# Second products of the last block with w2 as the stationary operand and 512 tokens streamed

## The chip, the cores and the metric

One Trainium2 chip, one of its cores. The metric is the device time of one execution in microseconds, the median of several runs.

## The reference, cut to what matters

Linear attention (its output is `x`, 2304 tokens by 512) and then a dense mixture of four experts:

```python
p = domain_probs / (domain_probs.sum(-1, keepdims=True) + 1e-09)
out = np.zeros((N, D), dtype=np.float32)          # 2304 x 512
for e in range(E):                                 # 4 experts
    h = np.maximum(x @ w1[e], 0.0)                 # 512 -> 1024
    out += p[:, e:e + 1] * (h @ w2[e])             # 1024 -> 512
```

All of it is float32. Each factor of a product is kept as a high and a low part of a narrower type (`hh`, `hl`), and a product is the sum of three: high by high, and the two mixed ones.

## The kernel before

The tokens go in blocks through the experts. The last block has 1024 tokens (`BIG[2]`, tokens 1280 to 2303); it makes eight visits (`DEEP`), each to one half (512 hidden features) of one expert. Attention is over by then. In this block both matrix products of a visit are cut into two by two parts, and seven products of parts stand for eight (Strassen's scheme in Winograd's form); the sums of parts that it needs are made by the other engines.

A visit, in the function `fast` with `deep` true:

- First products (`product`, L991, matmul at L999). The hidden features of the visit come in two halves `g` of 256, and for each there are seven products `p` of w1's parts with the token halves: six matmuls each (two slices of the sum, three pairs of high and low), w1 stationary in the array, 512 tokens streamed. The result is 128 features by 512 tokens in one PSUM bank. There are 84 matmuls a visit.
- Sums and relu. Some products are copied to SBUF by ScalarE (`keep`, L1005) and added by VectorE to later ones (`both`, L1013). The result goes through relu into the high part `hh` (ScalarE, L1023, L1057) and the low part `hl` (VectorE, L1029, L1060: relu and difference in one instruction). For the second seven products, differences of relu outputs are needed (`less`, L989, tiles `t1`, `t2` and `r11`), which are split into high and low by ScalarE and GpSimd (`split`, L630, L633).
- Second products (`sevens` at L1079, `seventh` at L1072, matmul at L1077). Here the hidden values are stationary, 128 tokens at a time, and 256 columns of w2 (or of sums of its parts, `w2s`) are streamed: each of the seven products has four token quarters `q`, two features slices `f` and three pairs, 24 matmuls of 256 columns, 168 a visit. Four banks `X` hold the left and right half of an output, two banks `Z` the third product. A result is 128 tokens by 256 output columns.
- `gather` (L830) adds a result to the output kept in SBUF (`acc`): VectorE multiplies by the share `pr` of the expert, which is one number for each partition (a token), and adds (L847; at first L843). In the last visit `finished` (L852) stores each piece of 128 by 256 at once.

Around this run, in the order in which they are written: the splits of w2's parts and of their sums for this and the next visit (`prepare`, `on_sides2`, on ScalarE and GpSimd), the loads of w2 (`load_deep`, L624, on SP's queue) and the loads of the next w1 parts from a kept copy (on GpSimd's queue). PSUM has eight banks, given out by `bank`. All engines work through their instructions in the order in which the function writes them; semaphores are put in for every dependence, and where two engines touch one PSUM bank, also between two readers.

Of the kernel before, what the change touches and what calls it, by code (L numbers as in the profile page):

```python
# [6 lines left out]
F32 = mybir.dt.float32  # L7
# [7 lines left out]
def attention_moe(ctx, tc, kT, qT, kd, qd, kn, qn, vn, omT, probs, w1, w2, out):  # L15
# [31 lines left out]

    raw_x = xs.tile([P, NP, RING], F32, tag="raw_x", name="raw_x")
# [60 lines left out]
    wide = {}  # L109
    cut = slice(D - 1, D - 1 + VW)  # L110
# [202 lines left out]
    class Halves(Pair):  # L313
# [87 lines left out]
        def turn(self, part):  # L401
# [7 lines left out]
            if part:  # L409
                pt = bank("qt_ps")[:, :P]  # L410
                nc.tensor.transpose(pt, self.qx[2][:, 0], ident)
                pieces.append((pt.rearrange("p (j t) -> p j t", j=2), slice(2 * P, 2 * P + D)))
# [409 lines left out]
    begun_at = set()  # L822

    def part(i, cs):
        if not isinstance(acc[i], list):
            return acc[i][:, cs]
        h = cs.start // H
        return acc[i][h][:, cs.start - h * H:cs.stop - h * H]

    def gather(v, ps, t, cs=slice(0, DM)):  # L830
        _, e, _, c0, n = visits[v]
        i = c0 // P + t
        sc = pr[:, i, e:e + 1]
        if i not in acc:
            if v in DEEP and t == 3:
                acc[i] = [att.tile([P, H], F32, tag=x, name="acc", bufs=1) for x in ("kvh", "kvl")]
            else:
                acc[i] = held([P, DM], "acc", F32)
        to = part(i, cs)
        fresh = [h for h in (0, H) if cs.start <= h < cs.stop and (i, h) not in begun_at]  # L840
        begun_at.update((i, h) for h in fresh)
        if fresh and v in DEEP:
            nc.vector.tensor_scalar(to, ps, sc, None, ALU.mult)  # L843
        elif fresh:
            nc.scalar.activation(to, ps, AF.Copy, scale=sc)
        else:
            nc.vector.scalar_tensor_tensor(to, ps, sc, to, ALU.mult, ALU.add)  # L847

    def finished(v, t, cs):
        if v + 1 == len(visits):  # L850
            i = visits[v][3] // P + t
            nc.sync.dma_start(out[i * P:(i + 1) * P, cs], part(i, cs))  # L852
# [104 lines left out]
    def fast(v):  # L957
# [3 lines left out]
        deep = v in DEEP  # L961
        hs = [tuple(held([P, n if deep else 2 * n], x) for x in ("hh", "hl")) for _ in range(FH)]
# [3 lines left out]
        ready2 = iter(())  # L966
# [3 lines left out]
        if deep:  # L970
            if v == DEEP[0]:
                sevens_t.append(xs.tile([P, 5, 2, n], F32R, tag="raw_x", name="t_hl"))
                for _ in range(2):
                    on_sides2(v)
            B, ready2 = sides2.pop(v)
            steps2 = [1, 0, 1, 0, 1, 1, 1, 0] if v == DEEP[0] else [1, 1, 1, 0, 0, 1, 1, 0]
            T1, A22 = ((sevens_t[0][:, i], sevens_t[0][:, i + 1]) for i in (0, 2))
            t1, t2 = (x.rearrange("p t c -> p (t c)")[:, :2 * n].rearrange("p (k x) -> p k x", k=2) for x in (va, vb))
            r11 = att.tile([P, 2, n], F32, tag="q", name="r11", bufs=1)

        def prepare():
            if deep:
                for _ in range(steps2.pop(0)):
                    next(ready2, None)
            else:
                split_w2()

        def less(to, t, x, op=ALU.subtract):
            nc.vector.scalar_tensor_tensor(to, t, 0.0, x, ALU.max, op)  # L989
# [19 lines left out]
        def both(g, f, j, where, name, hold=False):  # L1009
            t, kept = P_[g][where], P_[g][name]  # L1010
            if not deep or where == "u":
                t = kept
            nc.vector.tensor_tensor(t, P_[g][where], kept, ALU.add)  # L1013
            P_[g][name] = t
            if deep and j == 1:
                if g == 0:
                    if f == 0:
                        less(t1[:, 0], t, r11[:, 0])
                    return
                ha, hc = (x[:, f] for x in A22)  # L1020
            else:
                ha, hc = (x[:, j * n:(j + 1) * n] for x in hs[2 * g + f])
            nc.scalar.activation(ha, t, AF.Relu)  # L1023
            if deep and g == f == j == 0:
                nc.scalar.activation(r11[:, 0], t, AF.Relu)
            lows.append((hc, t, ha))
            if not (hold and not deep):
# [26 lines left out]
        def p4(g):  # L1054
# [3 lines left out]
            if deep and g == 0:  # L1058
                nc.scalar.activation(r11[:, 1], P_[0]["u"], AF.Relu)
# [12 lines left out]
        def seventh(q, to, a, b, start=True, fs=(0, 1)):  # L1072
            for f in fs:
                (xa, xc), (wa, wc) = a[f], b[f]
                xa, xc = (x[:, q * P:(q + 1) * P] for x in (xa, xc))
                for k, (x, w) in enumerate(((xa, wa), (xa, wc), (xc, wa))):
                    nc.tensor.matmul(to, x, w, start=(start and f + k == 0), stop=(f + k == 3), skip_group_check=not start)  # L1077

        def sevens():  # L1079

            L, R, Q = slice(0, H), slice(H, DM), range(4)

            def split_of(t):
                return [tuple(x[:, f] for x in t) for f in range(2)]

            def weights(g, cs):
                return [tuple(x[:, cs] for x in W[v, "w2", 2 * g + f]) for f in range(2)]

            def mixed(i, cs):
                return [tuple(x[:, cs] for x in B[f, i]) for f in range(2)]  # L1090

            X, Z = [], []
            for f in range(2):
                for q in Q[:2]:
                    if f == 0:
                        X.append(bank("g2"))
                    seventh(q, X[q][:, L], hs[:2], weights(0, L), fs=(f,))
            p7(1)
            less(t2[:, 1], P_[1]["p5"], t1[:, 1])
            for q in Q[2:]:  # L1100
                X.append(bank("g2"))
                seventh(q, X[q][:, L], hs[:2], weights(0, L))
            split(t2[:, 1], *hs[1], nc.scalar, nc.gpsimd)
            p3(1)
            p4(1)
            less(t2[:, 0], P_[1]["u2"], t1[:, 0])
            split(t2[:, 0], *hs[0], nc.scalar, nc.gpsimd)
            nc.gpsimd.tensor_tensor(r11, t2, r11, ALU.subtract)
            for q in Q:
                seventh(q, X[q][:, R], split_of(T1), mixed(1, R), start=False)  # L1110
            for q in Q:
                gather(v, X[q][:, L], q, L)
                gather(v, X[q][:, R], 4 + q, R)
            yield 2
            zs = []
            for q in Q:
                if q % 2 == 0:
                    Z.append(bank("g2"))
                zs.append(Z[q // 2][:, q % 2 * H:(q % 2 + 1) * H])
                seventh(q, zs[q], hs[2:], weights(1, L))  # L1120
            for f in range(2):
                split(r11[:, f], *hs[2 + f], nc.scalar, nc.gpsimd)
            yield 2
            for q in Q:
                seventh(q, X[q][:, R], split_of(A22), mixed(1, L), start=False)

            def second(q):
                gather(v, zs[q], q, L)
                finished(v, q, L)

            def third(q):
                gather(v, X[q][:, R], 4 + q, L)

            less(t1[:, 1], P_[1]["u"], t2[:, 1])
            less(t1[:, 0], P_[1]["p1"], t2[:, 0])
            for q in Q:
                third(q)
            for q in Q[:2]:
                second(q)
            split(t1, *T1, nc.scalar, nc.gpsimd)  # L1140
            next(ready, None)
            next(ready, None)
            on_sides2(v + 1)
            yield 1
            for q in Q:
                seventh(q, X[q][:, L], hs[:2], mixed(0, L), start=False)
                gather(v, X[q][:, L], 4 + q, L)
                finished(v, 4 + q, L)
                if q < 2:
                    second(2 + q)  # L1150
            next(ready, None)
            on_sides2(v + 1)
            on_sides2(v + 1)
            yield 1
            for q in Q:
                seventh(q, X[q][:, L], hs[2:], mixed(0, R), start=False)
                gather(v, X[q][:, L], 4 + q, R)
                finished(v, 4 + q, R)
# [6 lines left out]
            for t in range(tiles):  # L1165
                gathered(v, t)
# [386 lines left out]
```

## Time and profile before

| | us |
|---|---|
| median of 3 runs (lowest, highest) | 879.42 (878.98, 879.53) |
| the profiled execution | 879.01 |
| its span, first to last instruction | 877.2 |
| TensorE busy | 871.1 (99%), granted clock 1.00 |
| weight loads busy | 785.1 (90%) |
| VectorE, ScalarE, GpSimd busy | 568.1, 477.9, 563.9 |
| the last block, eight visits and the end | 560.4 to 877.2 |

The profile is of one execution. A busy time is a sum over an engine's instructions; matmuls overlap, so TensorE's says only that something was in flight. A wait is the idle time of an engine ahead of an instruction, put down to the one that released it last.

### The profile page before, as it was taken

The numbers are of one execution on the slowest core, as the hardware profiler recorded it, in microseconds if no ns is written. First come the engines' busy times: TensorE is split into PE (matmuls) and PEld (weight loads), VectorE is DVE, ScalarE is ACT, GpSimd is POOL, SyncE is SP. The second block draws the span as 40 slices with busy tenths as digits, with TensorE's granted clock in tenths as the row PEclk, the third lists the DMA queues.
The fourth block names the chain that finished last, engine by engine and source line by source line (L and its number), as shares of the span: only waits on it lengthen the run. The fifth ranks groups of instructions, "written<-read, shape, count | busy, mean of one in ns | idle before, by whom it ended". The sixth has DMA issues, their size and how long they took to land.

```text
span 877.2 us, 14757 instructions
## 1 busy us (share of the span) xinstructions
PE 871.1 (99%) x5456; PEld 785.1 (90%) x5456; DVE 568.1 (65%) x1001; ACT 477.9 (54%) x1075; POOL 563.9 (64%) x518
## 2 busy tenths in 40 slices
PE   9999999999999999999999999999999999999997
PEld 9988888989888898988989989898989899998987
DVE  5666566666678547566675666975847567574846
ACT  6696677776774555555555554544443434444341
POOL 6859474655644454444453436879888897889864
PEclk9999999999999999999999999999999999999999
DMA  7664534624421955645466255635144442515222
GB/s 183 194 211 159 204 111 155 187 77 144 159 73 49 314 182 202 232 139 192 142 214 226 82 197 227 214 112 180 44 174 121 131 136 81 171 47 180 80 89 97
DMA packets 64296, 134.01 MB, mean 153 GB/s; under 512 B 10368, under 2 KB 20800, under 8 KB 64224
## 3 DMA queue, kind: packets, MB, share of 16 engines
q1 hardware_dynamic: 54256, 102.95, 35.3%
q0 software_dynamic: 9360, 29.82, 10.4%
q8 instruction: 43, 0.70, 0.4%
q10 hardware_dynamic: 608, 0.30, 0.1%
q14 instruction: 29, 0.24, 0.1%
HBM read 98.96 MB, written 34.08 MB: 152 GB/s over the span
## 4 chain that ended last, share of the span: by engine, by line
PE 98%; DVE 1%; DMA 0%; issue 0%; ACT 0%; SPq 0%
PE g L999 31%; PE g L1077 18%; PE g L818 9%; PE g L819 8%; PE g L820 8%; PE g L803 3%; PE g L804 3%; PE g L805 3%; PE kv L396 2%; PE k_ps L341 2%; PE q_ps L341 1%; PE qt_ps L407 1%; PE k_ps L148 1%; PE q_ps L148 1%; PE nd L280 1%; PE kv L183 1%
## 5 line engine op out<-in xcount | busy, mean ns | idle before, releaser
L847 DVE SCALAR_TENSOR_TENSOR acc<-g,pr,acc 128x256 f32<-128x256 f32 (+1 forms) x278 | 140.2, 542 | 42.8 <-PE g L820 27.6
L633 POOL TENSOR_TENSOR w2l<-w2r,w2h 128x512 fp32r<-128x512 f32 x61 | 79.3, 1309 | 76.7 <-ACT w2h L630 66.4
L633 POOL TENSOR_TENSOR w1sl<-w1r,w1sh 128x512 fp32r<-128x512 f32 (+1 forms) x43 | 75.2, 1749 | 59.5 <-ACT w1sh L630 53.2
L818 PE MATMUL g<-w2h,hh 128*128 128x512 f32 x280 | 111.6, 399 | 0.0
L820 PE MATMUL g<-w2h,hl 128*128 128x512 f32 x280 | 109.6, 391 | 0.0
L819 PE MATMUL g<-w2l,hh 128*128 128x512 f32 x280 | 109.5, 391 | 0.0
L999 PE MATMUL g<-xbh,w1sh 128*128 128x384 f32 (+1 forms) x256 | 93.0, 363 | 0.0
L999 PE MATMUL g<-xbl,w1sh 128*128 128x384 f32 (+1 forms) x256 | 92.9, 363 | 0.0
L999 PE MATMUL g<-xbh,w1sl 128*128 128x384 f32 (+1 forms) x256 | 92.6, 362 | 0.0
L1005 ACT ACTIVATE sum<-g 128x384 f32<-128x384 f32 (+1 forms) x96 | 52.1, 543 | 69.5 <-PE g L999 68.6
L633 POOL TENSOR_TENSOR w1al<-w1r,w1ah 128x512 fp32r<-128x512 f32 (+1 forms) x45 | 49.5, 1116 | 59.6 <-ACT w1ah L630 56.2
L999 PE MATMUL g<-xbh,w1ah 128*128 128x384 f32 (+1 forms) x192 | 69.9, 364 | 0.0
L999 PE MATMUL g<-xbl,w1ah 128*128 128x384 f32 (+1 forms) x192 | 69.6, 362 | 0.0
L999 PE MATMUL g<-xbh,w1al 128*128 128x384 f32 (+1 forms) x192 | 69.5, 362 | 0.0
L1013 DVE TENSOR_TENSOR sum<-g,sum 128x384 f32<-128x384 f32 (+1 forms) x64 | 37.4, 587 | 44.1 <-PE g L999 38.8
L820 PEld LDWEIGHTS g<-w2h,hl 128*128 128x128 f32 x280 | 52.5, 188 | 11.5 <-DVE hl L810 0.2
L818 PEld LDWEIGHTS g<-w2h,hh 128*128 128x128 f32 x280 | 52.6, 188 | 10.2
L819 PEld LDWEIGHTS g<-w2l,hh 128*128 128x128 f32 x280 | 52.6, 188 | 8.9
L999 PEld LDWEIGHTS g<-xbh,w1sh 128*128 128x128 f32 x256 | 48.1, 188 | 5.7 <-DVE sum L1013 0.6
L999 PEld LDWEIGHTS g<-xbl,w1sh 128*128 128x128 f32 x256 | 48.1, 188 | 5.2
L1023 ACT ACTIVATE hh<-sum 128x384 fp32r<-128x384 f32 x48 | 25.0, 524 | 50.7 <-DVE sum L1013 50.3
L999 PEld LDWEIGHTS g<-xbh,w1sl 128*128 128x128 f32 x256 | 48.1, 188 | 5.1
(234 smaller groups left out, 2485.6 us busy)
## 6 DMA issues: line engine op xcount, KB each, us to landing
w1r<-in_w SPq DMA_DIRECT2D x54, 512.0 KB, 3.7
w2r<-in_w SPq DMA_DIRECT2D x76, 256.0 KB, 3.1
kept<-w1sh SPq DMA_DIRECT2D x16, 512.0 KB, 4.8
kept<-w1sl SPq DMA_DIRECT2D x16, 512.0 KB, 5.3
w1sh<-kept POOLq DMA_DIRECT2D x16, 512.0 KB, 4.8
w1sl<-kept POOLq DMA_DIRECT2D x16, 512.0 KB, 5.7
kept<-w1ah SPq DMA_DIRECT2D x16, 384.0 KB, 4.7
kept<-w1al SPq DMA_DIRECT2D x16, 384.0 KB, 4.8
```

Source lines behind the costliest of these rows:

```text
L341: nc.tensor.matmul(ps[j][:, i * P:(i + 1) * P], t[rows, c:c + P], om_r[rows], start=True, stop=True)
L633: lo.tensor_tensor(c, t, f32(a), ALU.subtract)
L803: nc.tensor.matmul(ps[:, :n], a[:, w], hi, start=(hp == 0), stop=False)
L804: nc.tensor.matmul(ps[:, :n], a[:, w], lo, start=False, stop=False)
L818: nc.tensor.matmul(ps, ha[:, ts_], wa, start=(c == 0), stop=False)
L819: nc.tensor.matmul(ps, ha[:, ts_], wc, start=False, stop=False)
L820: nc.tensor.matmul(ps, hc[:, ts_], wa, start=False, stop=(c == FH - 1))
L847: nc.vector.scalar_tensor_tensor(to, ps, sc, to, ALU.mult, ALU.add)
L999: nc.tensor.matmul(ps, a[:, w], x[:, k], start=(start and k + at == 0), stop=(k == 1 and at == 2), skip_group_check=not start)
L1005: nc.scalar.activation(t, P_[g][where], AF.Copy)
L1013: nc.vector.tensor_tensor(t, P_[g][where], kept, ALU.add)
L1077: nc.tensor.matmul(to, x, w, start=(start and f + k == 0), stop=(f + k == 3), skip_group_check=not start)
```

## The change

In the last block the second products change sides: w2's parts (128 of their columns at a time) stand in the array and the hidden values of 512 tokens are streamed. Each of the seven products has two output slices `i`, two feature slices `f` and three pairs, 12 matmuls of 512 columns, 84 a visit. A result is 128 output columns by 512 tokens; products that are added stay in two banks (`xl` or `xr`), the third has two banks `z`.

As tokens now lie along the free axis, a share can't be one number for each partition. A visit multiplies the hidden values instead: after the sums, which now stay in PSUM (two in new banks), VectorE does relu and the multiplication by a tile of shares in one instruction (`scaled`), and the high part, the low part and the differences are made from that. The share tiles (512 tokens the same in all partitions) are loaded from a small table in DRAM on SP's queue, once for each expert (`share_rows`); the table is written during attention (`turn_shares`: a transposition, a copy, a store). `into` then only adds a result to the output in SBUF. The output of this block is stored turned, in pieces of 128 by 512, and the host puts it in order.

The visit has its own function, `deep`; the other visits keep `fast` without the branches for it. The order of products, sums and preparations is that of before but for what follows: b11 is multiplied before product (1,6), the two slices of the first second product stand before and after product (1,7), `r11` is taken in two halves, and b12 and b22 are split later.

```diff
+    def share_rows(e):
+        if not shares:
+            shares.extend(held([P, 512], "w2r", F32, "share") for _ in range(2))
+        for j, t in enumerate(shares):
+            rows = pr_rows.rearrange("(j i e) p -> j e i p", j=2, e=E)[j, e]
+            nc.sync.dma_start(t.rearrange("p (i c) -> p i c", c=P), rows.partition_broadcast(P))
...
+        def added(g, where, name, to=None):
+            t = P_[g][where] if to is None else to
+            nc.vector.tensor_tensor(t, P_[g][where], P_[g][name], ALU.add)
+            return t
+        def scaled(t, j):
+            nc.vector.scalar_tensor_tensor(t, t, 0.0, shares[j], ALU.max, ALU.mult)
...
+        def high(t, to):
+            nc.scalar.activation(to, t, AF.Copy)
+        def low(t, hi, to):
+            nc.vector.tensor_tensor(to, t, f32(hi), ALU.subtract)
+        def times(to, a, b, fs=(0, 1), start=True, at=(0, 1)):
+            for f in fs:
+                (xa, xc), (wa, wc) = a[f], b[f]
+                for i in at:
+                    ps, w = to[i], slice(i * P, (i + 1) * P)
+                    for k, (y, x) in enumerate(((wa, xa), (wa, xc), (wc, xa))):
+                        nc.tensor.matmul(
+                            ps, y[:, w], x, start=(start and f + k == 0), stop=(f + k == 3), skip_group_check=not start
+                        )
+        def into(ps, j, c, at=(0, 1)):
...
+                if fresh:
+                    nc.vector.tensor_copy(t, ps[i])
+                else:
+                    nc.vector.tensor_tensor(t, ps[i], t, ALU.add)
...
+        product(1, 1, "u")
+        keep(1, "u", "p1")
+        a11 = added(0, "b2", "p1")
+        scaled(a11, 0)
+        high(a11, hs[0][0])
+        high(a11, r11[:, 0])
+        low(a11, *hs[0])
+        prepare()
+        product(1, 2, "b2")
+        a12 = added(1, "b2", "p1")
+        scaled(a12, 0)
+        high(a12, hs[2][0])
+        low(a12, *hs[2])
+        prepare()
+        product(0, 7, "u", start=False)
+        a21 = added(0, "u", "p5", bank("t"))
+        scaled(a21, 1)
...
+        product(0, 3, "b5", start=False)
+        b21 = added(0, "b5", "u2")
+        scaled(b21, 1)
+        product(0, 4, "u", start=False)
+        b11 = P_[0]["u"]
+        scaled(b11, 0)
+        high(b11, hs[1][0])
+        product(1, 6, "u", start=False)
+        keep(1, "u", "u2")
+        high(b11, r11[:, 1])
+        less(t1[:, 0], b21, r11[:, 0])
+        low(b11, *hs[1])
+        less(t1[:, 1], a21, r11[:, 1])
...
+        xl = [bank("g2") for _ in range(2)]
+        times(xl, hs[:2], weights(0, L), fs=(0,))
+        product(1, 7, "u", start=False)
+        a22 = added(1, "u", "p5", bank("t"))
+        scaled(a22, 1)
+        less(t2[:, 1], a22, t1[:, 1])
+        times(xl, hs[:2], weights(0, L), fs=(1,))
+        high(a22, A22[0][:, 1])
...
+        low(a22, A22[0][:, 1], A22[1][:, 1])
+        product(1, 3, "b5", start=False)
+        b22 = added(1, "b5", "u2")
+        scaled(b22, 1)
+        high(b22, A22[0][:, 0])
+        product(1, 4, "u", start=False)
+        b12 = P_[1]["u"]
+        scaled(b12, 0)
+        high(b12, hs[3][0])
+        less(t2[:, 0], b22, t1[:, 0])
...
+        low(b12, *hs[3])
+        low(b22, A22[0][:, 0], A22[1][:, 0])
+        xr = [bank("g2") for _ in range(2)]
+        times(xr, split_of(T1), mixed(1, R))
+        into(xr, 1, 1)
+        into(xl, 0, 0)
+        z = [bank("g2") for _ in range(2)]
+        times(z, hs[2:], weights(1, L))
...
+        times(xr, split_of(A22), mixed(1, L), start=False)
+        into(z, 0, 0)
+        done(0, 0)
+        into(xr, 1, 0)
...
+        times(xl, hs[:2], mixed(0, L), start=False)
+        into(xl, 1, 0)
+        done(1, 0)
...
+        times(xl, hs[2:], mixed(0, R), start=False)
+        into(xl, 1, 1)
+        done(1, 1)
...
+        for i in range(2):
+            times(xl, split_of(T1), weights(1, R), start=False, at=(i,))
+            into(xl, 0, 1, at=(i,))
+            done(0, 1, at=(i,))
```

## Rows read from the trace of the kernel before

**Rows 1.** Busy time by stretch, one visit: span; PE, PEld, DVE, ACT, POOL; PEclk; DMA.

```profile
599.40:638.40 39.00, 39.00 (x254) 35.66 (x253) 24.80 (x46) 16.46 (x28) 33.48 (x33) 1.00 0.39 130
```

**Rows 2.** Chain that ended last, one visit: start, length, engine, group, count.

```profile
599.56 14.99 PE g L999 x66
614.55 1.43 PE g L1077 x12
...
621.55 17.03 PE g L1077 x144
638.58 14.99 PE g L999 x66
```

**Rows 3.** VectorE in order, same visit: start, us, line, operation, [idle before <-releaser].

```profile
608.03 0.69 DVE L1029 SCALAR_TENSOR_TENSOR hl<-g,hh 128x512 fp32r<-128x512 f32 x1 [4.92 <-ACT r L1025]
608.64 0.69 DVE L1013 TENSOR_TENSOR g<-g,sum 128x512 f32<-128x512 f32 x1
609.99 0.69 DVE L1029 SCALAR_TENSOR_TENSOR hl<-g,hh 128x512 fp32r<-128x512 f32 x1 [0.66 <-ACT hh L1023]
610.60 0.68 DVE L1013 TENSOR_TENSOR sum<-g,sum 128x512 f32<-128x512 f32 x1
611.86 0.70 DVE L1013 TENSOR_TENSOR g<-g,sum 128x512 f32<-128x512 f32 x1 [0.58 <-PE g L999]
612.67 0.69 DVE L989 SCALAR_TENSOR_TENSOR va<-g,r 128x512 f32<-128x512 f32 x1
```

**Rows 4.** ScalarE in order, same visit.

```profile
606.42 0.60 ACT L1005 ACTIVATE sum<-g 128x512 f32<-128x512 f32 x1 [0.76 <-PE g L999]
...
607.39 0.60 ACT L1025 ACTIVATE r<-g 128x512 f32<-128x512 f32 x1
609.36 0.60 ACT L1023 ACTIVATE hh<-g 128x512 fp32r<-128x512 f32 x1 [1.36 <-DVE g L1013]
```

**Rows 5.** TensorE in order, same visit: the end of (0,3), the start of (0,4).

```profile
611.44 0.39 PE L999 MATMUL g<-xbh,w1sl 128*128 128x512 f32 x1
611.66 0.39 PE L999 MATMUL g<-xbh,w1ah 128*128 128x512 f32 x1
```

**Rows 6.** Groups by line and shape, last block: busy us, mean ns | idle before.

```profile
L847 DVE SCALAR_TENSOR_TENSOR acc<-g,pr,acc 128x256 f32<-128x256 f32 x208 | 89.2, 478 | 15.1 <-PE g L1077 15.1
...
L1013 DVE TENSOR_TENSOR sum<-g,sum 128x512 f32<-128x512 f32 x15 | 10.3, 686 | 11.1 <-PE g L999 11.1
...
L989 DVE SCALAR_TENSOR_TENSOR vb<-sum,va 128x512 f32<-128x512 f32 x8 | 6.0, 746 | 0.0
```

**Rows 7.** All engines in order, an earlier block: TensorE held by VectorE.

```profile
429.79 1.23 DVE L1013 TENSOR_TENSOR sum<-g,sum 128x384 f32<-128x384 f32 x2
429.91 0.33 PE L999 MATMUL g<-xbl,w1sh 128*128 128x384 f32 x1
...
430.08 0.34 PE L999 MATMUL g<-xbh,w1sl 128*128 128x384 f32 x1
...
430.39 0.19 PEld L999 LDWEIGHTS g<-xbh,w1sh 128*128 128x128 f32 x1 [0.29 <-DVE sum L1013]
...
430.68 0.34 PE L999 MATMUL g<-xbl,w1sh 128*128 128x384 f32 x1
```

**Rows 8.** VectorE in order, first visit of the last block: its first sum.

```profile
567.16 0.68 DVE L1013 TENSOR_TENSOR g<-g,sum 128x512 f32<-128x512 f32 x1
```

**Rows 9.** Waits of SP's queue, last block: total us, times, longest.

```profile
SPq L624 <- POOL w2l L633: 226.6, 7, 34.3
```

**Rows 10.** The end in order, then output stores: KB each, us to landing.

```profile
872.42 0.28 PE L1077 MATMUL g<-w2h,t_hl 128*128 128x256 f32 x1
872.74 0.48 DVE L847 SCALAR_TENSOR_TENSOR acc<-g,pr,acc 128x256 f32<-128x256 f32 x1 [0.23 <-PE g L1077]
...
out<-acc SPq DMA_DIRECT2D x10, 256.0 KB, 4.4
out<-acc SPq DMA_DIRECT2D x16, 128.0 KB, 1.9
```

More of the change, by code (lines that the diff above doesn't have):

```diff
@@ L820, in outputs, with gather @@
             nc.tensor.matmul(ps, hc[:, ts_], wa, start=False, stop=(c == FH - 1))
[L822 to L830, printed above, removed]
+    def gather(v, ps, t):
         _, e, _, c0, n = visits[v]
@@ L834, in gather @@
         if i not in acc:
[L835 to L845, printed above, removed]
-        else:
[L847 to L852, printed above, removed]
+            acc[i] = held([P, DM], "acc", F32)
+            nc.scalar.activation(acc[i], ps, AF.Copy, scale=sc)
+        else:
+            nc.vector.scalar_tensor_tensor(acc[i], ps, sc, acc[i], ALU.mult, ALU.add)
     def gathered(v, t):
@@ L960, in fast @@
         tiles, n = n // P, n // 2
-        deep = v in DEEP
-        hs = [tuple(held([P, n if deep else 2 * n], x) for x in ("hh", "hl")) for _ in range(FH)]
+        hs = [tuple(held([P, 2 * n], x) for x in ("hh", "hl")) for _ in range(FH)]
         P_ = [{}, {}]
@@ L1009, in both @@
         def both(g, f, j, where, name, hold=False):
[L1010 to L1022, printed above, removed]
+            t = P_[g][name]
+            nc.vector.tensor_tensor(t, P_[g][where], t, ALU.add)
+            ha, hc = (x[:, j * n:(j + 1) * n] for x in hs[2 * g + f])
             nc.scalar.activation(ha, t, AF.Relu)
-            if deep and g == f == j == 0:
-                nc.scalar.activation(r11[:, 0], t, AF.Relu)
             lows.append((hc, t, ha))
-            if not (hold and not deep):
+            if not hold:
                 for x, y, z in lows:
@@ L1070, in begun @@
             outputs(v, hs, g2[t], t, range(2))
[L1072 to L1158, printed above, removed]
-            on_sides2(v + 1)
-            yield 1
-            for q in Q:
-                seventh(q, X[q][:, L], split_of(T1), weights(1, R), start=False)
-                gather(v, X[q][:, L], q, R)
-                finished(v, q, R)
-            for t in range(tiles):
-                gathered(v, t)
-            yield 1
@@ L1192, in fast @@
         p5(1)
-        if deep:
-            prepare()
-            if v > DEEP[0] and v + 1 in DEEP:
-                start_sides2(v + 1)
         p3(0)
-        if u == 1:
-            keep_sides(v)
+        keep_sides(v)
         p4(0)
-        if deep:
-            less(t1[:, 1], P_[0]["p5"], r11[:, 1])
-            p6(1)
-            split(t1, *T1, nc.scalar, nc.gpsimd)
-            if v == DEEP[0]:
-                start_sides2(v + 1)
-            next(ready, None)
-            yield from sevens()
-            return
```

157 lines of the change are left out of this document (120 added, 37 removed).

## The prediction

> **What bounds the kernel now.** Read first the busy time by stretch, for one visit of the last block [rows 1]: TensorE is busy for all 39.00 us, at the full granted clock (1.00, the 2.4 GHz level), while VectorE works 24.80, ScalarE 16.46 and GpSimd 33.48. Then the chain of waits over the same visit [rows 2]: nothing but matrix products, 39.02 us from one visit's start to the next (599.56 to 638.58), eight visits alike. So a visit is as long as its row of matmuls, as long as every operand is there in time. The cost of a matmul is its distance to the next, not its busy time: 66 first products of 512 columns take 14.99 us, 0.2271 each; 12 second products of 256 columns take 1.43 and 144 take 17.03, 0.119 and 0.1183 each [rows 2] (a second stretch of 12 takes 1.43 too). Last, the times of VectorE, ScalarE and TensorE in the middle of a visit [rows 3 to 5], because the change lengthens the chain that runs through them. Product (g,p) is below the p-th first product of hidden half g, six matmuls; a11, a12, a21, a22, b11 and so on are the sums of first products, xl, xr and z the pairs of banks of the second products.
>
> **Part 1: what TensorE wins.** The 168 second products of 256 columns cost 1.43 + 1.43 + 17.03 = 19.89 us a visit. Their place is taken by 84 of 512 columns. With all 168 matmuls of a visit at 0.2271 it lasts 38.15 us, 0.87 less than 39.02; times eight visits, 6.96 us. The products' own groups alone give 19.89 - 84 x 0.2271 = 0.81 a visit, 6.5; that is the lower bound. What is won is the fixed part of each matmul, since the columns streamed are the same.
> The Trainium skill ("TensorE: Matmul & The Clock Gate", section Back-to-back issue gap) gives the distance as N/2.4 + 2.5 ns, so 109.2 and 215.8 ns here. By that estimate a visit would win only 168 x 0.1092 - 84 x 0.2158 = 0.22 us, 1.7 in all, and the sum below would end at 892.8. The rows above show a fixed part several times as large, and the measurement decides.
>
> **Part 2: VectorE's work.** Out go 28 gathers of 128x256 a visit at 0.478; in come 14 additions of 128x512 at 0.686 [rows 6] and eight multiplications by the shares, which read and write PSUM. The trace of before doesn't show these; the nearest rows are the additions with one operand in PSUM, 0.69 [rows 3], and as the upper end a sum of two SBUF tiles, 0.746 [rows 6]; I take 0.69. In total VectorE gains 28 x 0.478 = 13.4 and pays 14 x 0.686 + 8 x 0.69 = 15.1 us: far from 39. What matters is where the eight lie: between a sum and its high part, where the next engine waits. The pace of VectorE's queue is 0.61 from start to start (608.03, 608.64), 0.81 where the second needs the first's result (611.86, 612.67) [rows 3].
>
> **Part 3: the wait of product (0,4).** VectorE works through the low part of a11, the sum a12, its low part, the sum a21, in that order. Now they stand at 608.03, 608.64, 609.99 and 610.60 [rows 3]. The first is held until ScalarE's second copy out of the same bank (607.39, 0.60) is over, although it needs only the first copy; ScalarE itself first waits for product (1,1) (606.42) [rows 4]. None of that moves. Behind a12's sum now comes its multiplication: 608.64 + 0.81 = 609.45, over at 610.14. ScalarE takes the high part 0.03 later, as it does now (sum over at 609.33, copy at 609.36 [rows 3, 4]), for 0.60; the low part starts at 610.80 and a21 at 611.41, over at 612.09. Product (0,4) adds to the bank that a21 reads and must wait for it. Its first matmul stands at 611.66 [rows 5]. From the end of VectorE's instruction to a matmul that waits for it I take 0.14: in an earlier block TensorE waits for the first of two sums that begin at 429.79 and last 1.23 together, so it is over at about 430.37; the matmul after the held one is at 430.68, and with the distance of 0.17 there (429.91, 430.08) the held one ran as from 430.51 [rows 7]. So (0,4) begins at 612.23, **0.57 late**.
>
> **Part 4: the wait of the third second product.** At that product six of the eight banks are held (a12, b12, the two of xl, the two of xr), so its two are the last that came free: those of a22 and b22. From (0,4) on seven groups of six matmuls at 1.363, twelve of xr and three of z's first bank lead to 612.23 + 9.54 + 2.73 + 0.68 = 625.18, where b22's bank is wanted. VectorE gets a22's product at 612.23 + 4 x 1.363 + 0.19 = 617.87 (a product is seen 0.42 after its last matmul starts: 611.44 and 611.86 [rows 3, 5]). It is hardly free before: b11's low part waits for a copy that stands on ScalarE behind one that waits for product (1,6). Then sum, multiplication, difference at 617.87, 618.68, 619.49; ScalarE's copy until 620.81; a22's low part 620.84, b22's sum 621.45, its multiplication 622.26, ScalarE's copy until 623.58; the difference 623.61, b12's low part 624.22, b22's 624.83, over at 625.52. With the 0.14 z's second bank starts at 625.66, **0.48 late**.
>
> **Part 5: two banks handed over.** In the last three products the same two banks, xl, are added to, read out and added to again. Before, four banks of quarters were used, so a quarter had 18 matmuls of 0.118 to be read in. After, from the last matmul of xl's first bank to the next that writes it lie four steps, 4 x 0.2271 = 0.91. The reading needs 0.42 + 0.69 + 0.14 = 1.25: **0.34 late**, twice a visit, 0.68. The second bank is free in time.
>
> **Part 6: the rest.** The first visit pays 0.8 more: its first sum starts only at 567.16 [rows 8], so the multiplication is over at 568.66, later than ScalarE's copy can start now, and the whole chain of part 3 slides. The shares' table: one more transposition, shorter than a matmul of 512 columns, 0.1 to 0.2, and its copy and the small store lie beside products. The loads of the shares have no row: they stand on SP's queue ahead of the next w1r load, which waits up to 34.3 us there anyway [rows 9]; they wait for a multiplication in mid visit and are wanted after the next visit's start, over 10 us later, against 1.9 to 4.4 for a transfer of 128 or 256 KB [rows 10]. I take 0, and 2 us in all as the upper end. The end: the last matmul starts at 872.42 and its sum 0.32 later, 0.48 long [rows 10]; after, 0.42 and 0.69, 0.31 more. The last store has 256 KB, not 128: between 1.9 and 4.4 us, the latter beside other traffic [rows 10]; I take 0.4 more, in all 0.7, up to 2.8.
> GpSimd keeps its work, 33.48 of 39.00 us [rows 1]; only r11 is taken in two halves. I count nothing for it: what it splits comes later by as much as the products that want it, since both follow the same wait of part 3.
>
> **Sum.** Against the profiled execution, span 877.2, time 879.01 (the median of the runs is 879.42, so 0.4 of the difference to it is spread): -6.96 + 8 x (0.57 + 0.48 + 0.68 = 1.73) = -6.96 + 13.84, + 0.8 + 0.1 + 0.7, gives **887.5 us**, 1.0% slower.
>
> **The rivals.**
> A, no new waits: VectorE's chain keeps ahead, because low parts wait only for the copy that they need and dependent steps follow at 0.61, and TensorE's reading wait is covered. Place: product (0,4). It decides where a21 is read by 611.52, 0.57 earlier than in part 3. Then only the win is left: 879.0 - 6.96 + 1.6 = 873.7, faster. Against it: the wait for the second copy, 4.92 us up to 608.03, and the step of 0.81 both stand in the trace [rows 3].
> B, only the handover of part 5 stays: -6.96 + 16 x 0.34 + 0.8 = 878.3, no change. For it: parts 3 and 4 hang on sums of many steps, part 5 on three numbers.
> C, the multiplications cost 0.75 (two operands, GpSimd busy beside them): some fourteen steps of the chain, 0.06 each, 0.8 a visit, 894.
> D, the shares come late or the store form is slow: 2 to 3 us on top, inside the forecast's own range.
>
> **How the numbers follow.** The forecast with D has 0.75, its own range 883 to 892: the three waits may each be off by 0.1 a visit (8 x 0.3 = 2.4), with the bounds of part 1 and part 6. A has 0.09, B 0.08, C 0.08. Leaving out A and the top of C, the range is 878 to 893. What a measurement of this kernel can tell from no change is about 0.2%, 1.8 us: faster 0.11 (A and a little of B), same 0.08, slower 0.81.
>
> **What would show it.** In the profile after: second products 0.226 to 0.230 apart, in three groups by visit; TensorE idle before the first matmul of (0,4) and of z's second bank, and before xl's first bank twice, each put down to VectorE, 0.3 to 0.6 long; visits of about 39.9 us, the first 40.7; the granted clock still 1.00. I am wrong if these idle times are missing (A), if only the xl ones are there (B), or if VectorE's multiplications take much more than 0.69 (C); and part 1 is wrong if the distance of second products isn't near 0.227.

## The result, and the profile after

The changed kernel takes 887.55 us (median of five runs, 886.90 to 887.83), the kernel before, on the same chip, 879.42 (878.98 to 879.63). The ratio is 1.0092, with a 95% interval of 1.0078 to 1.0107: slower by a little under 1%. The profiled run took 887.46 us with a span of 885.7; the prediction was 887.5. Of the kernel called slices below, one of ten executions ran at a granted clock of 0.65 and took 1233.03 us; it is left out, and that kernel's trace comes from a second run.

The first view is again busy time by stretch, one visit of the changed kernel beside the one of [rows 1] (span; PE, PEld, DVE, ACT, POOL; PEclk; DMA):

```profile
681.03:720.97 39.94, 39.32 (x169) 31.23 (x169) 25.86 (x40) 16.55 (x28) 32.67 (x33) 1.00 0.48 134
```

TensorE is no longer busy for the whole visit: 39.32 of 39.94 us, at the same granted clock of 1.00. VectorE has 25.86 instead of 24.80, in fewer instructions; ScalarE (16.55) and GpSimd (32.67) are about where they were. By the shares of busy time nothing has happened; what is new is that 0.62 us of a visit shows as idle, and that the matmuls around each idle time run further apart than elsewhere.

The second view is the chain that ended last through the same visit, in the places of [rows 2]:

```profile
681.03 6.82 PE g L1115 x30
...
688.36 0.59 ACT hh L1135
688.95 0.50 ACT r L1135
...
689.47 0.69 DVE hl L1138
690.16 0.62 DVE g L1125
...
690.80 0.71 DVE g L1129
...
691.53 0.61 ACT hh L1135
...
692.17 0.69 DVE hl L1138
692.86 0.62 DVE t L1125
...
693.52 3.06 PE g L1115 x12
...
703.38 10.58 PE g L1146 x45
...
713.98 0.70 DVE acc L1160
...
714.82 2.32 PE g L1146 x9
...
717.16 0.70 DVE acc L1160
...
718.00 2.97 PE g L1146 x12
```

In the kernel before this chain was nothing but matrix products. Now it leaves TensorE three times in a visit. From 687.85 (681.03 + 6.82) to 693.52 it runs through ScalarE's copies and VectorE's low part of a11, sum and multiplication (L1129) of a12, low part of a12 and sum of a21, and ends at product (0,4). At 713.98 and at 717.16 it goes through VectorE's sum out of xl's first bank (L1160). Six visits run from 601.15 to 840.75, 39.93 each, against 39.02 before.

How much each wait takes is read from TensorE's own row, as the distance of two matmuls less the usual 0.227:

```profile
692.88 0.39 PE L1115 MATMUL g<-xbh,w1sl 128*128 128x512 f32 x1
693.52 0.50 PE L1115 MATMUL g<-xbh,w1ah 128*128 128x512 f32 x1 [0.25 <-DVE t L1125]
693.86 0.40 PE L1115 MATMUL g<-xbl,w1ah 128*128 128x512 f32 x1
...
706.43 0.40 PE L1146 MATMUL g<-hh,w2l 128*128 128x512 f32 x1
706.79 0.50 PE L1146 MATMUL g<-hh,w2h 128*128 128x512 f32 x1
707.13 0.40 PE L1146 MATMUL g<-hl,w2h 128*128 128x512 f32 x1
...
713.55 0.62 PE L1146 MATMUL g<-hh,w2s 128*128 128x512 f32 x2
...
714.24 0.40 PE L1146 MATMUL g<-hh,w2s 128*128 128x512 f32 x1
714.82 0.47 PE L1146 MATMUL g<-hh,w2s 128*128 128x512 f32 x1 [0.18 <-DVE acc L1160]
715.12 0.40 PE L1146 MATMUL g<-hl,w2s 128*128 128x512 f32 x1
```

Product (0,4) starts 0.64 after the matmul ahead of it and its second matmul another 0.34 later: 0.41 + 0.11 = 0.52 lost. The second bank of z: 0.36 and 0.34, that is 0.13 + 0.11 = 0.24. xl: 0.58 and 0.30, 0.35 + 0.07 = 0.42, and by the same working 0.43 the second time (718.00). Together 1.61 us a visit. Note that the idle time that the row names, 0.25 and 0.18, is much less than what is lost, and that the wait for z's bank has no name at all; distances tell it, the bracket doesn't.

Three instructions of VectorE's row, for the account further down: the sum of a21, the sum of a22 and the low part of b22.

```profile
692.77 0.69 DVE L1125 TENSOR_TENSOR t<-g,sum 128x512 f32<-128x512 f32 x1
...
699.33 0.70 DVE L1125 TENSOR_TENSOR t<-g,sum 128x512 f32<-128x512 f32 x1 [0.25 <-PE g L1115]
...
706.06 0.68 DVE L1138 TENSOR_TENSOR t_hl<-g,t_hl 128x512 fp32r<-128x512 f32 x1
```

VectorE's instructions by line and shape, last block (busy us, mean ns | idle before), answer [rows 6]:

```profile
L1160 DVE TENSOR_TENSOR acc<-g,acc 128x512 f32<-128x512 f32 x104 | 67.6, 684 | 37.1 <-PE g L1146 37.1
L1129 DVE SCALAR_TENSOR_TENSOR g<-g,share 128x512 f32<-128x512 f32 x48 | 31.9, 696 | 1.1
```

The multiplication, which no row of before showed, takes 0.70; the 16 on a21 and a22 have a row of their own with 699.

Where the 8.5 us of span are (885.7 against 877.2): the second visit starts at 601.15, before at 599.56 [rows 2], 1.59 later; six visits more at 39.93 instead of 39.02 are 5.48; the last visit with the end takes 885.7 - 840.75 = 44.95 instead of 877.2 - 833.68 = 43.52, 1.43 more, of which 0.91 is again the visit and 0.51 the end in this execution. 1.59 + 5.48 + 1.43 = 8.50.

### The profile page after: what moved, and what is told of

The parts are those of the page before. It is cut to its first block, busy times and chain, and to the rows that moved or that the text cites. A ratio compares the mean times of both kernels' runs of the same rounds, so it can differ in the third digit from the quotient of the medians.

```text
span 885.7 us, 13361 instructions
## 1 busy us (share of the span) xinstructions
PE 873.5 (99%) x4785; PEld 749.6 (85%) x4785; DVE 578.4 (65%) x953; ACT 478.4 (54%) x1076; POOL 561.4 (63%) x526
## 4 chain that ended last, share of the span: by engine, by line
PE 89%; DVE 6%; ACT 2%; issue 2%; DMA 1%; SPq 0%; DVEq 0%
PE g L1146 17%; PE g L967 13%; PE g L1115 12%; PE g L830 8%; PE g L831 8%; PE g L832 8%; PE g L815 3%; PE g L816 3%; PE g L817 3%; PE kv L406 2%; PE k_ps L351 1%; DVE acc L1160 1%; PE q_ps L351 1%; PE qt_ps L417 1%; DVE xbl L645 1%
## 5 line engine op out<-in xcount | busy, mean ns | idle before, releaser
L1160 DVE TENSOR_TENSOR acc<-g,acc 128x512 f32<-128x512 f32 x104 | 67.6, 684 | 37.1 <-PE g L1146 37.1
L842 DVE SCALAR_TENSOR_TENSOR acc<-g,pr,acc 128x512 f32<-128x512 f32 x70 | 51.0, 735 | 28.0 <-PE g L832 27.9
L1121 ACT ACTIVATE sum<-g 128x512 f32<-128x512 f32 x48 | 28.6, 595 | 61.5 <-PE g L1115 61.5
L645 POOL TENSOR_TENSOR w2s<-w2f,w2s 128x512 fp32r<-128x512 f32 x30 | 38.3, 1302 | 25.7 <-ACT w2s L642 25.7
L645 POOL TENSOR_TENSOR t_hl<-va,t_hl 128x1024 fp32r<-128x1024 f32 x16 | 38.7, 2422 | 20.6 <-ACT t_hl L642 20.6
L303 DVE RECIPROCAL dn<-dn 128x256 f32<-128x256 f32 (+1 forms) x24 | 46.5, 1943 | 6.7 <-ACT dn L297 6.2
L1115 PE MATMUL g<-xbh,w1sh 128*128 128x512 f32 x128 | 49.9, 390 | 0.0
L1115 PE MATMUL g<-xbl,w1sh 128*128 128x512 f32 x128 | 49.9, 389 | 0.0
L1115 PE MATMUL g<-xbh,w1sl 128*128 128x512 f32 x128 | 49.8, 389 | 0.0
L645 POOL TENSOR_TENSOR w2l<-w1r,w2h 128x512 fp32r<-128x512 f32 x32 | 44.1, 1391 | 6.5 <-ACT w2h L642 6.4
```

The source lines that it names most:

```text
L303: nc.vector.reciprocal(dn, dn)
L645: lo.tensor_tensor(c, t, f32(a), ALU.subtract)
L842: nc.vector.scalar_tensor_tensor(acc[i], ps, sc, acc[i], ALU.mult, ALU.add)
L1115: nc.tensor.matmul(ps, a[:, w], x[:, k], start=(start and k + at == 0), stop=(k == 1 and at == 2), skip_group_check=not start)
L1121: nc.scalar.activation(t, P_[g][where], AF.Copy)
L1160: nc.vector.tensor_tensor(t, ps[i], t, ALU.add)
```

## The experiments

The theory: the wider matmuls win about 0.8 us a visit, and three kinds of waits of TensorE for VectorE, 1.6 us together, take that back twice over. The rivals: VectorE's added work, or the multiplication, costs as such wherever it lies; the loads of the shares cost; the wider matmul wins little. Each experiment is timed against the kernel before on its own chip, so ratios are compared, at 879.4 us each 0.001 being 0.88 us. The visits are the mean distance of visit starts in the profile from the second to the last.

| kernel | ratio to before (95%) | visit, us |
|---|---|---|
| before | 1 | 39.02 |
| changed | 1.0092 (1.0078 to 1.0107) | 39.93 |
| a12's low part later | 1.0046 (1.0033 to 1.0060) | 39.38 |
| b22's low part first | 1.0076 (1.0062 to 1.0090) | 39.72 |
| slices | 1.0016 (1.0007 to 1.0026) | 39.06 |
| all three | 0.9940 (0.9928 to 0.9953) | 38.24 |
| a11's second copy later | 1.0055 (1.0041 to 1.0069) | 39.51 |
| shares loaded once | 1.0094 (1.0080 to 1.0107) | 39.93 |
| no multiplications | 1.0010 (1.0000 to 1.0020) | 39.13 |
| all three, end in halves | 0.9941 (0.9929 to 0.9953) | 38.24 |
| all three, matmuls of 256 columns | 0.9994 (0.9985 to 1.0003) | 38.97 |

**A12's low part later.** One line of VectorE's work moves behind two others.

```diff
         high(a12, hs[2][0])
-        low(a12, *hs[2])
 ...
         a21 = added(0, "u", "p5", bank("t"))
         scaled(a21, 1)
+        low(a12, *hs[2])
```

> The edit: VectorE takes a21's sum and multiplication ahead of a12's low part, nothing else moves. Theory (three kinds of waits of TensorE for VectorE eat the win): in the changed kernel a12's low part stands at 692.17, held until ScalarE's copy is over, and a21's sum only behind it at 692.77; product (0,4) loses 0.52 a visit, 0.97 in the first. Now a21's sum follows a12's multiplication (690.80) at about 691.4, over at 692.1, and (0,4) was due at about 693.0: the idle time there goes, visits take 39.42 instead of 39.94, the time 7 x 0.52 + 0.97 = 4.6 less, 883. The waits at z's second bank and at xl stay. Rival 1 (VectorE's added work costs as such, wherever it lies): the same instructions in another order, 887.5. Rival 2 (the low part that comes later delays a second product): the gain is given back, 886 to 888.

Measured: 882.5 us, the ratio down by 0.0046, 4.0 us; visits of 39.38, 0.55 shorter. VectorE in order, one visit:

```profile
687.97 0.69 DVE L1138 TENSOR_TENSOR hl<-g,hh 128x512 fp32r<-128x512 f32 x1 [4.19 <-ACT r L1135]
688.58 0.69 DVE L1125 TENSOR_TENSOR g<-g,sum 128x512 f32<-128x512 f32 x1
689.30 0.70 DVE L1129 SCALAR_TENSOR_TENSOR g<-g,share 128x512 f32<-128x512 f32 x1
689.91 0.69 DVE L1125 TENSOR_TENSOR t<-g,sum 128x512 f32<-128x512 f32 x1
...
691.24 0.68 DVE L1138 TENSOR_TENSOR hl<-g,hh 128x512 fp32r<-128x512 f32 x1
```

The sum of a21 comes 1.94 after a11's low part, in the changed kernel 3.30 (689.47 to 692.77). The chain through product (0,4) is an unbroken row of 66 first products again (14.96 us). The same instructions, in another order, are worth the whole wait: rival 1 is out for this part, and no second product is late for it.

**B22's low part first.**

```diff
-        low(b12, *hs[3])
         low(b22, A22[0][:, 0], A22[1][:, 0])
+        low(b12, *hs[3])
```

> The edit: b22's low part stands ahead of b12's on VectorE. Theory: the third second product's second bank is b22's, free only when its low part (706.06, 0.68 long) is over; TensorE loses 0.24 there a visit (706.79). One step of 0.61 earlier, the bank is free at 706.1, before it is wanted: 8 x 0.24 = 1.9 less, 885.6, visits 39.70. Rival: the bank was held by something else, or b12's low part, which z's second half of products wants 1.36 after the first, is late now: 887.5 or more.

Measured: 885.15, the ratio down by 0.0016, 1.4 us, which the two intervals alone don't tell apart. The visits do: 39.72, 0.22 shorter, against the 0.24 expected, and TensorE's row at z's second bank is even (0.24, where it was 0.36):

```profile
706.31 0.40 PE L1146 MATMUL g<-hh,w2l 128*128 128x512 f32 x1
706.55 0.39 PE L1146 MATMUL g<-hh,w2h 128*128 128x512 f32 x1
```

So it was b22's bank, and b22's low part that held it.

**Slices.** Two second products are taken one output slice after the other.

```diff
-        times(xl, hs[:2], mixed(0, L), start=False)
-        into(xl, 1, 0)
-        done(1, 0)
+        for i in range(2):
+            times(xl, hs[:2], mixed(0, L), start=False, at=(i,))
+            into(xl, 1, 0, at=(i,))
+            done(1, 0, at=(i,))
```

and the same for `hs[2:], mixed(0, R)` with `into(xl, 1, 1)`.

> The edit: the last but one and the one before it of the second products run one output slice after the other (six matmuls, then that bank's sum), as the last one does already; the number of matmuls is unchanged. Theory: from a bank's last matmul to the next that writes it lie then seven steps of 0.227, 1.59, or more instead of four, 0.91; the handover takes 0.42 + 0.69 + 0.14 = 1.25, so both waits at xl (0.42 and 0.43 a visit in the changed kernel) go: 8 x 0.85 = 6.8 less, 880.7, visits 39.09. Rival (the handover waits for VectorE's other work, not for the distance): VectorE's sums come one by one instead of in pairs, the waits shrink by half at most, 884 or more.

Measured: 880.18, the ratio down by 0.0076, 6.7 us. The trace is that of a second run of the same kernel.

> The same kernel as the slices run (880.18), for a trace at the full granted clock. Theory: TensorE's waits for VectorE's sums of xl are gone, the ones at (0,4) (0.5 a visit) and at z's second bank (0.24) stand as in the changed kernel, visits 39.09. Rival: some of the xl wait is left, visits 39.3 or more, and the rest was won elsewhere.

Measured: 879.78 us in one run, clock 1.00, visits of 39.06, 0.87 shorter (0.85 expected). The chain, one visit:

```profile
639.40 6.81 PE g L1115 x30
...
651.89 3.06 PE g L1115 x12
...
661.75 16.72 PE g L1146 x72
```

The 72 second products at a visit's end are one piece; the two detours through L1160 are gone, and the one ahead of (0,4) is still there (between 646.21 and 651.89). VectorE's sums now start every 1.36 us and wait for TensorE, not the other way round.

**All three.**

> The edit: the three of the other runs of this call together (a21's sum ahead of a12's low part; b22's low part ahead of b12's; two second products slice by slice). Theory: the waits add up and nothing else is late, so what is left is the win of the wider matmuls alone: 168 matmuls at 0.2271 to 0.2275 a visit are 38.2; 8 x (0.52 + 0.24 + 0.85 = 1.61) + 0.45 for the first visit's longer wait = 13.3 less, 874.2, below the kernel before by 5.2. Rival 1 (another wait comes up behind the three: GpSimd's low parts, or the splits of T1, which now are wanted earlier): 877 to 881. Rival 2 (the wider matmul wins only what the fixed part of 2.5 ns would give, 0.22 a visit): 879.4 or more, and second products more than 0.23 apart.

Measured: 873.27 us, ratio 0.9940: 13.4 us below the changed kernel by the ratios, and 0.6% faster than the kernel before. One visit by busy time, and its chain:

```profile
676.08:714.32 38.24, 38.24 (x169) 31.54 (x169) 25.76 (x40) 16.64 (x28) 32.60 (x33) 1.00 0.45 140
```

```profile
676.08 14.96 PE g L1115 x66
...
697.84 16.48 PE g L1146 x72
```

TensorE is busy for all of it again. The three moves alone gave 0.55 + 0.22 + 0.87 = 1.64 a visit, together 1.69: they add up, and no fourth wait stands behind them. VectorE's work (25.76) is what it is in the changed kernel; it costs nothing once it is out of the way. What is left against the kernel before is the win of the wider matmuls, 39.02 - 38.24 = 0.78 a visit. The first visit gains little: from its first matmul to the next visit's it takes 38.83 (560.61 to 599.44), in the kernel before 39.00 (560.40 to 599.40). There TensorE's weight loads wait 0.5 for GpSimd and 0.3 for ScalarE.

**A11's second copy later.** The first link of the chain of part 3 by itself.

```diff
-        high(a11, r11[:, 0])
         low(a11, *hs[0])
+        high(a11, r11[:, 0])
```

> The edit: ScalarE's second copy of a11 (into r11) is issued after VectorE's low part of a11, so that the low part need not come after it; nothing else moves. Theory of part 3's first link: a11's low part (689.47 in the changed kernel, after 4.18 of idle time) is held by ScalarE's second read of the same bank, one copy of 0.60 longer than it needs; without that VectorE's row up to a21's sum begins some 0.5 earlier and the 0.52 idle time before product (0,4) shrinks to about 0: 883 like the run that moved a12's low part (882.5). Rival: the low part waits for the first copy, which itself waits for product (1,1)'s copy on ScalarE, and the second copy only appears to release it: 887.5, (0,4) as late as before. A second possibility on the same edit: the copy now waits for the low part and delays the high part of a12 on ScalarE, so that the gain goes back: 886 to 887.5.

Measured: 883.68, the ratio down by 0.0037, 3.3 us; visits of 39.51, 0.42 shorter. ScalarE's two copies of a11, and VectorE's low part, in the changed kernel (first fence) and here (second fence):

```profile
688.36 0.59 ACT L1135 ACTIVATE hh<-g 128x512 fp32r<-128x512 f32 x1
688.84 0.60 ACT L1135 ACTIVATE r<-g 128x512 f32<-128x512 f32 x1
...
689.47 0.69 DVE L1138 TENSOR_TENSOR hl<-g,hh 128x512 fp32r<-128x512 f32 x1 [4.18 <-ACT r L1135]
```

```profile
687.42 0.59 ACT L1135 ACTIVATE hh<-g 128x512 fp32r<-128x512 f32 x1
688.12 0.69 DVE L1138 TENSOR_TENSOR hl<-g,hh 128x512 fp32r<-128x512 f32 x1 [3.77 <-ACT hh L1135]
688.90 0.60 ACT L1135 ACTIVATE r<-g 128x512 f32<-128x512 f32 x1 [0.89 <-DVE hl L1138]
```

With the second copy ahead the low part starts 1.11 after the first copy's start, without it 0.70. It was held by a read of the same bank whose result it doesn't use, as part 3 had it. The rest of the wait, 0.1 a visit, is still there. The second copy now waits for the low part, but this delays nothing: ScalarE's high part of a12 still starts 0.03 after its multiplication ends (690.15, 690.18).

**Shares loaded once.**

```diff
-        if v in DEEP[1::2] and not last:
-            share_rows(visits[v + 1][1])
```

> The edit: the table of shares is loaded once, in the first visit of the last block, and not again for the other three experts (those then use wrong shares; that is the part of the computation that it changes). Six loads of 256 KB on SP's queue are gone. Theory of part 6: the loads stand beside work that nobody waits for, 887.5. Rival D: they come late or hold up the w1 loads behind them on the queue, up to 2 us in all: 885.5 to 886.5.

Measured: 886.92, ratio 1.0094 where the changed kernel has 1.0092, visits of 39.93. The six loads, 5.0 us each from issue to landing in the changed kernel, cost nothing that the visits or the intervals show. Rival D of this expectation is out.

**No multiplications.** `scaled` does nothing.

```diff
         def scaled(t, j):
-            nc.vector.scalar_tensor_tensor(t, t, 0.0, shares[j], ALU.max, ALU.mult)
+            pass
```

> The edit: VectorE's eight multiplications a visit are left out (relu and shares are missing from this kernel's output; the loads of the shares stay). Theory: in the changed kernel they cost nothing as work, only by the two waits they lie ahead of: product (0,4) comes in time (0.52 a visit, 0.97 in the first) and z's second bank is free in time (0.24), while both waits at xl (0.42, 0.43) stay as they are: 8 x 0.24 + 4.6 = 6.5 less, 881.0, visits 39.18. Rival C (the multiplications hold up the kernel as a whole, xl's reading included): the xl waits shrink too, towards 874. Rival: the waits hang on VectorE's longer additions of 512 columns, not on the multiplications: 885 or more.

Measured: 879.55, the ratio down by 0.0082, 7.2 us, against 6.5 expected; visits of 39.13, 0.80 shorter. The chain, one visit:

```profile
639.04 14.96 PE g L1115 x66
...
660.80 10.36 PE g L1146 x45
672.03 2.32 PE g L1146 x9
675.21 2.97 PE g L1146 x12
```

The waits at (0,4) and at z's second bank are gone, the two at xl stand as they did: 45, 9 and 12 second products, with 0.87 and 0.86 of detour through L1160 between the pieces. So eight multiplications of 0.70 cost the changed kernel 0.8 us a visit and not 5.6, all by the two places in which they lie; and xl's wait has nothing to do with them. This refutes rival C of this expectation. With all three moves, where VectorE does the same work and TensorE doesn't wait, it also rules out VectorE's load as such as the cause.

**All three, matmuls of 256 columns.** The disputed gain by itself: the kernel with all three moves, with 78 of a visit's 84 second products issued in two halves.

```diff
-                        nc.tensor.matmul(ps, y[:, w], x, ...)
+                        for cs in ((slice(0, n),) if start and f + k == 0 else (slice(0, n // 2), slice(n // 2, n))):
+                            nc.tensor.matmul(ps[:, cs], y[:, w], x[:, cs], ...)
```

> The edit, on top of the kernel with all three moves (873.3): each second product's matmul of 512 columns that doesn't begin a bank (78 of 84 a visit) is issued as two of 256 columns with the same weights tile; the columns, the order, VectorE's work and the waits stay. Theory of part 1: only the fixed part of a matmul differs, 2 x 0.1183 - 0.2271 = 0.0095 each, 78 x 0.0095 = 0.74 a visit, 5.9 in all: 879.2, visits 38.98 instead of 38.24. Rival (the Trainium skill, TensorE: Matmul & The Clock Gate, section Back-to-back issue gap: a fixed part of 2.5 ns): 78 x 2.5 ns = 0.2 a visit, 1.6 in all, 874.9. Rival 2 (a second matmul with the same weights doesn't pay for its weights again): below 874.9.

Measured: 878.34, ratio 0.9994, 4.7 us more than all three by the ratios; visits of 38.97, 0.73 longer (0.74 expected). The chain, one visit:

```profile
638.89 14.99 PE g L1115 x66
...
660.85 17.01 PE g L1147 x140
```

That is the visit of the kernel before, 39.02, to 0.05. The 4.7 us are less than 8 x 0.73 = 5.8. The first visit, which waits for others, ends only 0.32 later (599.92), so the visits make 7 x 0.73 + 0.32 = 5.4; the rest is within the two intervals. Rival 2 is out as well: a pair of halves takes two weight loads and gets no cheaper by having the same weights (4785 weight loads in the kernel with all three, 5409 here).

The Trainium skill ("TensorE: Matmul & The Clock Gate", section Back-to-back issue gap) gives a gap of N/2.4 + 2.5 ns, by which, as an estimate, this run would be 0.2 a visit dearer; the trace shows 0.73, over three times as much. The same section of the Trainium skill calls that formula the gap of a single, isolated matmul and says that at 512 columns it gives more than a row of weight loads and matmuls takes. The prediction left that condition out, and the rows here, with a weight load for each matmul, go the other way: 227 ns at 512 columns, where the formula gives 216.

**All three, end in halves.** In the last visit the last slice is taken in two halves of 256 tokens, with a sum and a store for each.

```diff
-            times(xl, split_of(T1), weights(1, R), start=False, at=(i,))
-            into(xl, 0, 1, at=(i,))
-            done(0, 1, at=(i,))
+            for cs in ((slice(0, n // 2), slice(n // 2, n)) if last and i else (slice(0, n),)):
+                times(xl, split_of(T1), weights(1, R), start=False, at=(i,), cs=cs)
+                into(xl, 0, 1, at=(i,), cs=cs)
+                done(0, 1, at=(i,), cs=cs)
```

> The edit, on top of the kernel with all three moves (873.3): in the last visit the last output slice of the last product is taken in two halves of 256 tokens, each with its own sum of 128x256 and its own store of 128 KB. Theory of part 6's end: from the start of the last sum to the end of the span lie 4.98 (867.32 to 872.3), where the kernel before has 4.46 with a sum and a store of half the size; the halves cost 6 x (2 x 0.1183 - 0.2271) = 0.06 of matmuls more, so 0.5 - 0.06 = 0.4 less, 872.8. Rival (two small stores on one queue end no earlier than one large one): 873.3.

Measured: 873.65, ratio 0.9941 where all three have 0.9940: no gain is seen, though the intervals, 0.0012 to each side, couldn't tell 0.4 us from nothing. The end, in order:

```profile
866.27 1.14 DVE L1160 TENSOR_TENSOR acc<-g,acc 128x512 f32<-128x512 f32 x2 [0.67 <-PE g L1146]
...
866.66 0.28 PE L1146 MATMUL g<-t_hl,w2l 128*128 128x256 f32 x1
867.46 0.50 PE L1146 MATMUL g<-t_hl,w2h 128*128 128x256 f32 x2 [0.52 <-DVE acc L1160]
...
868.47 0.42 DVE L1160 TENSOR_TENSOR acc<-g,acc 128x256 f32<-128x256 f32 x1 [1.07 <-PE g L1146]
```

The second half's matmuls wait for VectorE's sum of the first half, 0.80 from one matmul to the next instead of 0.12, although they write other columns: it is the same bank. That loses 0.68 where 0.4 was to be won. I had made the wait that the whole study is about, and not seen it. The rival's reason is not what the trace shows: from the start of the last sum (868.47) to the end of the span (871.7) lie 3.2, less than in any run with the larger sum and store. Nor was 4.98 a safe start for the theory: the same end took 3.64 to 4.14 in seven other profiles and 4.95 in the changed kernel's.

## Why the prediction was right, step by step

Each of the four waits stood where it was forecast, in the order forecast, and three runs that change one order each take them away one by one: the mechanism was right. That the time was met to 0.1 us is luck. The terms were less exact than their sum, as the parts below show, and the sum started from the profiled execution (879.01); between the medians lie 8.13 us, where the sum has 8.5. One sign failed as it was worded: TensorE's idle time ahead of the held matmuls was to be 0.3 to 0.6 and put down to VectorE each time, and the profile names 0.25 at (0,4), 0.18 at xl and nothing at z's second bank. There the distances, and the run with b22's low part first, show the wait.

**Part 1** was a little too large: 0.87 a visit was forecast, and all three moves leave 0.78, below the lower bound of 0.81. The first products are as forecast (14.96 for 66, 0.2267 each), the second products in the long stretch stand 16.48/72 = 0.2289 apart, where 0.2271 was taken from the first products' row. The 2 ns are not spread evenly: with all three moves 27 of the 72 stand 0.228 to 0.241 apart and the others at 0.2267 like the first products. What slows the 27 the runs don't tell.

**Part 2** held: 0.70 for a multiplication (0.69 taken), pace 0.61. The pace of dependent steps was wrong: 0.81 was read from one pair of [rows 3], in which the second instruction is of another kind and has a wait for GpSimd's semaphore as well; without such a wait a multiplication follows its sum by 0.72 (688.58 and 689.30 in the run with a12's low part later).

**Part 3**: 0.57 forecast, 0.52 measured. From a11's low part to a21's sum 3.38 were counted, 3.30 measured (689.47 to 692.77); that difference is the dependent step. The two runs that shorten this row, and the one without multiplications, each take the wait away, all but 0.1 in one of them.

**Part 4**: 0.48 forecast, 0.24 measured, the largest miss. The count from a22's sum to b22's low part was 6.96, the trace has 6.73 (699.33 to 706.06); the three dependent steps in it are 0.07 to 0.08 shorter each, and that is 0.23 of the 0.24 missing. The bank, the order and the instruction were right.

**Part 5**: 0.34 forecast, 0.42 and 0.43 measured. From the last matmul of xl's first bank (713.55) to VectorE's sum lie 0.43, the sum takes 0.70, and 0.14 later the next matmul starts: 1.27 in all, 1.25 counted. The rest is that the matmul after the held one comes 0.30 later instead of 0.227. The 0.14 taken from [rows 7] was worked out from the second matmul and was to hold that delay too. By the same working (the second matmul less 0.227, less the sum's end) it is 0.17 at (0,4), 0.16 at z's bank and 0.21 here: one figure for three places was too small, most of all here.

So the waits sum to 1.61 instead of 1.73, the win is smaller by 0.09, and the two errors cancel in a visit (39.93 against 39.88). **Part 6**: the first visit ends 1.59 later than before, -0.87 + 1.73 + 0.8 + 0.1 = 1.76 was forecast; its wait at (0,4) is 1.24 (572.38 to 573.74 to 574.07, less 0.227 twice), 0.72 above a later visit's, 0.8 forecast. The loads cost 0, as taken. The end costs 0.51 in this execution, 0.7 forecast: 0.21 for the sum, and from the sum's end to the span's end 4.28 (881.42 to 885.7) instead of 3.98. That the larger store costs these 0.3 is not shown. In the eight other profiles with the same last sum and store, 3.64 to 5.01 lie between the start of that sum and the span's end, against 4.95 here and 4.46 before: the end scatters by more than the term.

**The rivals.** A fell because VectorE's chain does depend on the second copy and on the multiplication, with 0.72 and not 0.61 between dependent steps. B would have been right without the multiplications: 878.3 was its price, and that kernel takes 879.55. C's multiplication of 0.75 takes 0.70, and the loads of D cost nothing that is seen. The forecast of the sign depended on the sum of parts 3 to 5 being more than 0.9 a visit; by the runs, the two xl waits alone (0.87 together by the slices) already outweigh the win (0.78).

## What to carry to other kernels

One matmul of 512 columns in place of two saves a fixed part, but it can also leave fewer steps between the last write of a bank and the next, here four of 0.227 where 18 of 0.118 had been, and that distance is what covers the other engine's read; order the products so that between a bank's last write and its next there are as many steps as the read takes (here 1.27 us, which needs six steps of 0.227). When work is put into the queue of an engine that has a third of its time free, ask only what stands behind it there: eight multiplications cost 0.8 us a visit where they were put, and nothing that is seen after two lines were moved. And after a change that came out slower, add up the distances between matmuls around each idle time: here they named three small moves that made the slower kernel the fastest of all, 0.994 of the kernel before.

## What the runs showed of the hardware

- After a wait, TensorE's next matmul follows the held one by 0.30 to 0.34 us and the ones behind it by 0.23 to 0.24, where 0.227 is usual: a wait costs 0.07 to 0.11 us more than the held matmul's own delay. Distances of 0.228 to 0.241 also stand where nothing is seen to wait, in 27 of 72 second products with all three moves.
- Two matmuls of 256 columns take 0.2366 together (2 x 0.1183), one of 512 columns 0.2267 to 0.2289: 8 to 10 ns for a split, in the kernel before and in the kernel with halves alike, though both halves have the same weights.
- A multiplication of two operands that reads and writes PSUM, 128x512, took 0.70 us, as long as a sum out of PSUM, and the next instruction on VectorE started 0.72 to 0.74 after the start of one whose result it needs, 0.61 after one whose result it doesn't.
- Two engines that touch the same bank were made to wait for each other by this program even where they touch other columns (0.80 instead of 0.12 at the end in halves), and even where both only read (the low part 1.11 after the copy's start instead of 0.70).
